# A chunked delta rule with two gated products: one row order, three inverse buffers, a lane inverse in one stream

## The chip, the core and the metric

The kernel runs on one core of a Trainium2 chip. The metric is the device time of one execution in microseconds; the time of a version is the median of several executions.

## What is computed

A delta-rule attention over 768 tokens for 4 x 8 pairs of batch and head (head size 48), then two dense products over its 3072 outputs of 384 numbers each.

```python
k_n = k / (norm(k, axis=-1) + 1e-06)
for t in range(768):
    y[t] = q[t] @ state
    v_old = k_n[t] @ state
    state = state + beta[t] * outer(k_n[t], v[t] - v_old)
xn = y / sqrt(mean(y * y) + 1e-6) * rms_g             # 3072 x 384
g = xn @ w_gate                                       # 384 x 1536
x = (silu(g) * (xn @ w_val)) @ w_out
h = x @ w_in                                          # 384 x 2048
out = (h * tanh(softplus(h))) @ w_out2
```

## The kernel before, in words

**Rows and segments.** The 768 tokens are cut into 12 rows `r` of 64 tokens, for all 32 pairs at once; two rows make a segment `sg`. In a row the recurrence is solved in closed form: a 64x64 unit-triangular matrix made of Gram products of the keys is inverted for each pair, and the row then needs matrix products alone. The state goes from row to row, so the rows follow each other. All this stands in `phase_b1`, which takes the first 510 us of the span. The two dense products behind it (phases b2 and c) are not edited.

**A row of the chain** (`chain_row`, L769). Its pieces have letters, and a table of letters gives their order on the engines:
- `r` `residual`: PE multiplies keys and state (L795), DVE subtracts that from v (L800).
- `q0`, `q1` turn q (PE L495, copied by ACT L496). `y` `of_state` is q by state (PE L813).
- `p` `scores`: q by keys (PE L478 into two PSUM banks), which DVE masks into `PT` (L487).
- `v` `values`: the inverse `A` by the residual (PE L832); ACT copies the result (L837).
- `k` `kv_update`: keys by values (PE L881); DVE adds them to the state `sx` (L886).
- `o0`, `o1` `outputs`: ACT, then POOL take mean square and root. Their other half belongs to the next row: `S`, `T` scale the output (`po`, DVE L893), `X`, `Y` (`to_x`) turn it on PE (L908), ACT copies it to `xh` and `xf` (L910, L913), and POOL makes the rest `xl` (L914). The tile of `xh` and `xl` is what the first dense product reads.
- `nA` is the norm of a later row's keys (square on ACT L418, sum `ss` on DVE L420, root `nr` on POOL L433 and L434); `nB` takes the reciprocal `rn` on DVE (L443) and scales the keys on POOL (`kh`, L444).
- `c0`, `c1` turn the normalized keys of row r+3 and `g` makes their Gram product into `A` (PE L478, masked by DVE L487); `d0`, `d1` and `h` do the same for row r+4.

Even rows follow `EVEN`, in which no `c`, `d`, `g`, `h` stands; odd rows follow `ODD`, which holds two Gram products; rows 0 and 1 have tables of their own.

**The inverse.** `inlane(sg)` (L499) inverts the 32x32 diagonal blocks of a segment's two rows at once on DVE, with some of the products on POOL (`prp`, both at L529). ACT and POOL copy the result into `A` (L601, L602). `merge32` (L608) then joins two 32-blocks to a 64-block by two PE products. `invert(sg)` runs `inlane` and then two `merge32`. It starts in an even row and ends in the next odd row; `PREP` and `SPLIT` say how much of it goes to which row. There are two `A` buffers; `As[sg % 2]` is taken again when `values` of row r-3 has read it.

**Part A** (`gated`, L205) is the first dense product for the first two of its pairs of weight slices, done beside the chain on the row before: nine-matmul pieces `up` (PE L201 to L203, the second matmul of each three reads `xl`), a gate on ACT, DVE and POOL (`sg` L242, `hh` L245, `hl` L246), and `down` (PE L218 to L220), whose sums ACT copies to `par` (L971).

**What sets the order.** `merge` (L32) interleaves the streams of a row (its chain, a budget of Part A given by `DUE`, weight conversions, the lane) by their planned weights; every engine then runs its instructions in the order in which they were issued. A wait on one engine so holds all that was issued behind it there.

Of the kernel before, what the change touches and what calls it, by code (L numbers as in the profile page):

```python
# [19 lines left out]
P = dict(  # L20
    XB=2, WE=16, RB=4, TB=3, PREP=42.0, SPLIT=0.40, XL=1, HH=0, DPRE=5, WU0=24, WU1=35, WARM=[0, 0], CVS=[2.6, 10.0, 2.5, 13.1, 0], CVA=12, CVT=12.22, CVB0=0, CVB1=1.238, CVC=2.31, PSD=1, INV=1, Q=[0, 2.7, 1.2, 9.9, 0, 18.8, 2.8, 3.0, 11.5, 10.6, 11.0, 19.4], W=[22, 2, 14, 8, 0, 14], SQ=1, QC=1, CVP=0, NE=2, BQ=3, NU=6, CVN=1, CVE=14.671, CVD=4.076, OFF=2.9, SOFT=0,
    EVEN="r nA S q0 T q1 X Y y v p nB k o0 o1".split(),
    ODD="r nA S q0 T q1 X Y y c0 v nB c1 p k g d0 o0 d1 o1 h".split(),
    R0="r q0 q1 p nA v o0 o1 s0 nB k s1 x0".split(),
    R1="r nA q0 Y q1 y p c0 v c1 nB k o0 o1 s1 g s0 d0 d1 x0 h".split(),
    DUE=[0, 4, 9, 10, 12],
    PRE="n2 t00 t01 w1 g0 s1 w2 s2 n3 t10 | t11 c g1 c c s3 t20 t21 | t30 g2 t31 w3 g3".split(),
# [31 lines left out]
def kernel(  # L59
# [133 lines left out]
    def need(*keys):  # L193
        assert done.issuperset(keys), set(keys) - done
# [72 lines left out]
    def phase_b1():  # L267
# [39 lines left out]
        kTs = [(kp if i in late_kT else il).tile([128, B, 2, 128], F32, name=f"kT{i}") for i in range(4)]  # L307
        As = [(kp if i == (NSEG - 1) % 2 else il).tile([128, 32, 64], F32, name=f"A{i}") for i in range(2)]
        qp = kp.tile([128, 16, 64], F32, name="qp")
# [151 lines left out]
        def products(r, soft=False):  # L461
            if r >= NR:
                return
            sg, rl = divmod(r, 2)
            if rl == 0:
                need(*([("v", r - 3)] if sg > 1 else []))
                A_t[sg] = As[sg % 2]
            need(("T", r, 0), ("T", r, 1))
            gram(("G", r), kT_t[r], kT_t[r], mneg, A_t[sg][:, rl * 16:rl * 16 + 16, :], soft, swap=True)
            yield 1  # L470
# [288 lines left out]

        def invert(sg):  # L760
            yield from inlane(sg)
            yield from delay(P["INV"])
            X11 = X11_t.pop(sg)
            Z = N_[:, 0:1024].rearrange("p (u c) -> p u c", c=32)
            for rl in range(2):
                us = slice(rl * 16, rl * 16 + 16)
                yield from merge32(2 * sg + rl, X11[:, us], Z[:, us])

        def chain_row(r):  # L769
# [129 lines left out]
            def to_x(bp):  # L899
# [154 lines left out]
        )  # L1054
        PREP = P["PREP"]
        SP = P["SPLIT"]
        M1A = 4.0 * FA + KD
        ps_ds = [ps_d]
        part_a = gated((ps_u, ps_ds, hp, tp), range(FA), range(NR), get_xa, finish_a, next_x)
        for sg in range(NSEG):  # L1060
            nxt = invert(sg + 1) if sg + 1 < NSEG else None
            for rl in range(2):
                r = 2 * sg + rl
                streams = [(chain_row(r) if r else chain0, cost(r))]
                due = P["DUE"][r] if r < len(P["DUE"]) else P["DUE"][-1 if r % 2 == 0 else -2]
                if due > 0:
# [208 lines left out]
```

## Time and profile before

| | |
|---|---|
| median of 3 runs | 1247.69 us (1244.75 to 1249.08) |
| profiled execution, its own time | 1247.47 us |
| its span | 1245.7 us |
| first phase, the chain's rows | to 510 us of the span |
| PE busy | 1118.6 us (90%) |
| DVE busy | 741.8 us (60%) |
| ACT busy | 510.1 us (41%) |
| POOL busy | 519.1 us (42%) |
| mean granted clock of TensorE | 0.934 of full speed |

Shares over the whole span mix two different parts. Behind 510 us the work is PE's alone; ahead of it PE and DVE take turns in setting the pace. So the rows below are cut by row of the chain. A row r begins with `residual` on PE: row 2 at 146.5 us, row 3 at 172.1, row 4 at 212.6, row 6 at 281.8, row 7 at 312.0, row 8 at 350.0, row 9 at 379.6, row 10 at 415.6. Where a timeline row ends in brackets, these hold the engine's idle time ahead of the instruction and what ended it.

### The profile page before, as it was taken

The numbers are of one execution on the slowest core, as the hardware profiler recorded it, in microseconds if no ns is written. First come the engines' busy times: TensorE is split into PE (matmuls) and PEld (weight loads), VectorE is DVE, ScalarE is ACT, GpSimd is POOL, SyncE is SP. The second block draws the span as 40 slices with busy tenths as digits, with TensorE's granted clock in tenths as the row PEclk, the third lists the DMA queues.
The fourth block names the chain that finished last, engine by engine and source line by source line (L and its number), as shares of the span: only waits on it lengthen the run. The fifth ranks groups of instructions, "written<-read, shape, count | busy, mean of one in ns | idle before, by whom it ended". The sixth has DMA issues, their size and how long they took to land.

```text
span 1245.7 us, 32276 instructions
## 1 busy us (share of the span) xinstructions
PE 1118.6 (90%) x14100; PEld 1083.2 (87%) x14100; DVE 741.8 (60%) x1133; ACT 510.1 (41%) x902; POOL 519.1 (42%) x441
## 2 busy tenths in 40 slices
PE   6575679888898887899999999997999999999998
PEld 5465568878787886899999999997999999999998
DVE  6999695868869598556555552269534333343333
ACT  3344324353443563221121110045655555565672
POOL 7256283655635355344434342234422322332232
PEclk9666689999999798899999999998999999999999
DMA  5224032333224354333343212332111011111101
GB/s 123 55 79 103 12 80 54 78 78 78 66 67 116 100 158 165 102 115 107 104 159 109 95 64 86 121 114 75 39 39 39 13 39 39 38 40 39 31 9 27
DMA packets 121438, 95.21 MB, mean 76 GB/s; under 512 B 80720, under 2 KB 103888, under 8 KB 121296
## 3 DMA queue, kind: packets, MB, share of 16 engines
q1 hardware_dynamic: 109200, 69.54, 19.8%
q10 hardware_dynamic: 12096, 23.60, 5.7%
q8 instruction: 111, 1.82, 0.6%
q14 instruction: 31, 0.25, 0.1%
HBM read 64.80 MB, written 28.31 MB: 75 GB/s over the span
## 4 chain that ended last, share of the span: by engine, by line
PE 69%; DVE 23%; issue 2%; ACT 2%; SPq 2%; POOL 1%; DMA 0%; DVEq 0%; POOLq 0%; ACTq 0%
PE pd L1171 5%; PE pd L1172 5%; PE pd L1170 5%; PE ph L201 5%; PE ph L202 5%; PE ph L203 5%; PE pv L201 4%; PE pd L218 4%; PE pg L201 3%; PE pd L219 3%; PE pg L203 3%; PE pg L202 3%; PE pd L220 3%; PE pv L203 3%; PE pv L202 3%; DVE pr L529 3%
## 5 line engine op out<-in xcount | busy, mean ns | idle before, releaser
L1218 POOL TENSOR_TENSOR gl<-t,gh 128x512 fp32r<-128x512 f32 x96 | 125.4, 1307 | 253.7 <-DVE gh L1217 252.3
L246 POOL TENSOR_TENSOR hl<-sg,hh 128x512 fp32r<-128x512 f32 x72 | 101.5, 1409 | 179.4 <-DVE hh L245 176.3
L201 PE MATMUL ph<-xh,wih 128*128 128x256 f32 x576 | 162.6, 282 | 4.6 <-DVE t L1214 4.6
L202 PE MATMUL ph<-xl,wih 128*128 128x256 f32 x576 | 162.4, 282 | 0.0
L203 PE MATMUL ph<-xh,wil 128*128 128x256 f32 x576 | 162.2, 282 | 0.0
L236 ACT ACTIVATE sg<-pg 128x512 f32<-128x512 f32 x72 | 43.1, 598 | 255.0 <-PE pg L203 218.0
L242 DVE TENSOR_TENSOR sg<-sg,pv 128x512 f32<-128x512 f32 x72 | 49.5, 687 | 151.6 <-PE pv L203 149.2
L218 PE MATMUL pd<-hh,woh 128*128 128x256 f32 x432 | 126.5, 293 | 7.7 <-ACT par L971 4.2
L1171 PE MATMUL pd<-wql,gh 128*128 128x384 f32 x384 | 130.4, 340 | 1.8 <-POOL wql L159 1.8
L1170 PE MATMUL pd<-wqh,gh 128*128 128x384 f32 x384 | 130.1, 339 | 1.7 <-DVE wqh L158 1.7
L1172 PE MATMUL pd<-wqh,gl 128*128 128x384 f32 x384 | 130.0, 339 | 0.0
L201 PE MATMUL pv<-xh,wvh 128*128 128x256 f32 x432 | 128.3, 297 | 0.0
L201 PE MATMUL pg<-xh,wgh 128*128 128x256 f32 x432 | 128.0, 296 | 0.0
L202 PE MATMUL pg<-xl,wgh 128*128 128x256 f32 x432 | 123.9, 287 | 2.5 <-POOL xl L914 2.5
L219 PE MATMUL pd<-hl,woh 128*128 128x256 f32 x432 | 123.2, 285 | 0.8 <-POOL hl L246 0.8
L203 PE MATMUL pv<-xh,wvl 128*128 128x256 f32 x432 | 123.9, 287 | 0.0
L202 PE MATMUL pv<-xl,wvh 128*128 128x256 f32 x432 | 123.8, 287 | 0.0
L203 PE MATMUL pg<-xh,wgl 128*128 128x256 f32 x432 | 123.8, 287 | 0.0
L220 PE MATMUL pd<-hh,wol 128*128 128x256 f32 x432 | 123.1, 285 | 0.0
L1214 DVE TENSOR_TENSOR t<-t,ph 128x512 f32<-128x512 f32 x96 | 65.2, 679 | 82.4 <-ACT t L1212 82.4
L201 PEld LDWEIGHTS ph<-xh,wih 128*128 128x128 f32 x576 | 109.6, 190 | 4.8 <-DVE t L1214 4.8
L202 PEld LDWEIGHTS ph<-xl,wih 128*128 128x128 f32 x576 | 109.5, 190 | 0.0
(197 smaller groups left out, 2951.6 us busy)
## 6 DMA issues: line engine op xcount, KB each, us to landing
raw<-in_moe_w_out_dram SPq DMA_DIRECT2D x28, 384.0 KB
raw<-in_moe_w_in_dram SPq DMA_DIRECT2D x16, 384.0 KB
kh<-in_k_dram SPq DMA_DIRECT2D x24, 192.0 KB
qp<-in_q_dram SPq DMA_DIRECT2D x24, 192.0 KB
v<-in_v_dram SPq DMA_DIRECT2D x48, 96.0 KB
raw<-in_moe_w_gate_dram SPq DMA_DIRECT2D x12, 384.0 KB
raw<-in_moe_w_val_dram SPq DMA_DIRECT2D x12, 384.0 KB
xh_d<-xh SPq DMA_DIRECT2D x12, 384.0 KB
```

Of the source, the lines that this page charges most:

```text
L201: nc.tensor.matmul(ps[:, f, :], wh[:, kt, sl], xh[:, kt, :], start=(kt == 0), stop=False)
L202: nc.tensor.matmul(ps[:, f, :], wh[:, kt, sl], xl[:, kt, :], start=False, stop=False)
L203: nc.tensor.matmul(ps[:, f, :], wl[:, kt, sl], xh[:, kt, :], start=False, stop=(kt == KD - 1))
L218: nc.tensor.matmul(ps, wh[:, f, sl], hh[:, f, :], start=(i + f == 0), stop=False)
L219: nc.tensor.matmul(ps, wh[:, f, sl], hl[:, f, :], start=False, stop=False)
L220: nc.tensor.matmul(ps, wl[:, f, sl], hh[:, f, :], start=False, stop=last)
L246: nc.gpsimd.tensor_tensor(out=hl, in0=sg, in1=hh.bitcast(F32), op=ALU.subtract)
L1170: nc.tensor.matmul(ps, gh[:, f, sl], wh[:, f, :], start=(m + f == 0), stop=False)
L1171: nc.tensor.matmul(ps, gh[:, f, sl], wl[:, f, :], start=False, stop=False)
L1172: nc.tensor.matmul(ps, gl[:, f, sl], wh[:, f, :], start=False, stop=last)
L1214: nc.vector.tensor_tensor(out=t, in0=t, in1=ps, op=ALU.mult)
L1218: nc.gpsimd.tensor_tensor(out=gl, in0=t, in1=gh.bitcast(F32), op=ALU.subtract)
```

## The change

Four edits, all in `phase_b1`:
- One table `ROW` orders rows 2 to 11. Each row turns the keys of row r+4 and makes one Gram product, and `R0` and `R1` do the same. In `ROW`, `nB` stands ahead of `X` and `Y`, `scores` stands far ahead of `kv_update`, scaling (`S`, `T`) stands some pieces ahead of turning (`X`, `Y`), and `values` follows `Y`.
- Three `A` buffers: the one of segment sg is taken again when `values` of row r-5 has read it. `comp`, the first tile of the lane inverse, moves to another tag with two buffers, and `Z` of the merges gets a tile of its own.
- `invert` becomes `merges` and one generator `lanes`, which runs the lane inverses of segments 2 to 5 one behind the other. The merges of a segment are stepped while the next segment's lane runs. Each row takes `LANE` = 16 of the stream's planned weight; the share in row 9 is 23 with no budget.
- Part A's budget per row becomes 4, 9, and 11 in every row from 3 on; before, it was 4, 9, then 10 and 12 by turns. Its last stretch behind the chain is planned at 20.0 for 21.0. The second of two copies of the lane's result on ACT is issued without a pause.

```diff
-    EVEN="r nA S q0 T q1 X Y y v p nB k o0 o1".split(),
-    ODD="r nA S q0 T q1 X Y y c0 v nB c1 p k g d0 o0 d1 o1 h".split(),
-    R0="r q0 q1 p nA v o0 o1 s0 nB k s1 x0".split(),
-    R1="r nA q0 Y q1 y p c0 v c1 nB k o0 o1 s1 g s0 d0 d1 x0 h".split(),
-    DUE=[0, 4, 9, 10, 12],
+    ROW="r nA q0 q1 S p T y nB X Y v c0 c1 k o0 g o1".split(),
+    R0="r q0 q1 p nA v o0 o1 s0 nB k s1 x0 c0 c1 g".split(),
+    R1="r nA q0 Y q1 y p nB v k o0 o1 s0 s1 x0 c0 c1 g".split(),
+    DUE=[0, 4, 9, 11],
...
-                need(*([("v", r - 3)] if sg > 1 else []))
-                A_t[sg] = As[sg % 2]
+                need(*([("v", r - 5)] if sg > 2 else []))
+                A_t[sg] = As[sg % 3]
...
-            comp = il.tile([128, 32, 32], F32, tag="X11", name="comp")
+            comp = il.tile([128, 1024], F32, tag="pr", name="comp", bufs=2).rearrange("p (u c) -> p u c", c=32)
...
             nc.scalar.copy(A[32:64, :, 32:64], Yc[32:64])
             nc.gpsimd.tensor_scalar(out=A[:, :, 0:32], in0=Yc, scalar1=h0[:, 0:1], scalar2=None, op0=ALU.mult)
+            nc.scalar.copy(A[96:128, :, 32:64], Yc[96:128])
             X11_t[sg] = X11
-            yield 2.0
-            nc.scalar.copy(A[96:128, :, 32:64], Yc[96:128])
-            yield 1.1
+            yield 0.1
...
+        def lanes():
+
+            ending = iter(())
+            for sg in range(2, NSEG):
+                done_of, due = 0.0, 4.0
+                for w in inlane(sg):
+                    yield w
+                    done_of += w
+                    if done_of >= due:
+                        next(ending, None)
+                        due += 2.5
+                for _ in ending:
+                    pass
+                ending = merges(sg)
+            yield from delay(P["INV"])
+            yield from ending
...
-                c0=lambda: turn_k(r + 3, 0), c1=lambda: turn_k(r + 3, 1),
-                g=lambda: products(r + 3), h=lambda: products(r + 4),
-                d0=lambda: turn_k(r + 4, 0), d1=lambda: turn_k(r + 4, 1),
+                c0=lambda: turn_k(r + 4, 0), c1=lambda: turn_k(r + 4, 1), g=lambda: products(r + 4),
...
-                elif nxt is not None:
-                    streams.append((budget(nxt, PREP * SP) if rl == 0 else nxt, PREP * (SP if rl == 0 else 1 - SP)))
+                elif sg + 1 < NSEG:
+                    pace = P["LANE"] if r < NR - 3 else 99.0
+                    streams.append((budget(lane, pace), P["LANE"] if r < NR - 3 else P["LANE"] + 7.0))
```

Lines of the changed kernel are 13 higher from `chain_row` on (L921 is the turn of x, L845 `values`, L894 `kv_update`, L927 `xl`), and one lower up to the lane's copies into `A` (L200 to L202 are `up`, L245 `hl`, L432 and L433 `nr`, L443 `kh`, L528 `prp`).

PE, an odd row (row 5), around the second turn of x. In a row read `out<-in`; `po` is the scaled output, `pg` and `pv` are the sums of Part A's `up`, and `wgh_1500` and `wvh_1682` belong to the block that Part A is already working on. Before; the first piece on the x tile just turned is the one with `wgh_886`:

```order
L908 MATMUL pp<-ident,po 128x128 x3
L813 MATMUL pp<-sx,QT 64x48 x32
L201 MATMUL pg<-xh,wgh_1500 128x256
...
L495 MATMUL pp<-ident,kh_173 128x128 x4
L832 MATMUL pp<-v,A_179 64x48 x32
L201 MATMUL pv<-xh,wvh_1682 128x256
...
L881 MATMUL pp<-ve_182,kh_170 64x48 x16
L201 MATMUL pg<-xh,wgh_886 128x256
L202 MATMUL pg<-xl,wgh_886 128x256
L203 MATMUL pg<-xh,wgl_887 128x256
```

The same place in the change, where the first piece on the new x tile has `wgh_887`:

```order
L921 MATMUL pp<-ident,po 128x128 x3
L845 MATMUL pp<-v,A_181 64x48 x32
L200 MATMUL pg<-xh,wgh_887 128x256
L201 MATMUL pg<-xl,wgh_887 128x256
L202 MATMUL pg<-xh,wgl_888 128x256
```

Between the second turn of x and the first read of the new tile stood four blocks of the chain (state, values, scores, `kv_update`), a turn of keys in two halves and three pieces of Part A; now `values` alone stands between them.

POOL, an odd row (row 5), from the norm of the keys or the products on, before (`prp` are lane products, `kh_174` are the keys, `hl` is Part A's rest):

```order
L529 TENSOR_TENSOR prp<-X__168,T_3528 128x512
L529 TENSOR_TENSOR prp<-X__168,T_3528 128x256
L433 TENSOR_TENSOR nr<-ss,half 128x16
L434 TENSOR_SCALAR nr<-nr 128x16
L914 TENSOR_TENSOR xl<-xf,xh 128x3x128 x2
L444 TENSOR_TENSOR kh_174<-kh_174,rn 128x16x48
L246 TENSOR_TENSOR hl<-sg,hh 128x512
```

And in the change:

```order
L432 TENSOR_TENSOR nr<-ss,half 128x16
L433 TENSOR_SCALAR nr<-nr 128x16
L528 TENSOR_TENSOR prp<-X__168,T_3545 128x512
L528 TENSOR_TENSOR prp<-X__168,T_3545 128x256
L443 TENSOR_TENSOR kh_174<-kh_174,rn 128x16x48
L927 TENSOR_TENSOR xl<-xf,xh 128x3x128
L245 TENSOR_TENSOR hl<-sg,hh 128x512
L927 TENSOR_TENSOR xl<-xf,xh 128x3x128
```

The two halves of `xl` stood behind `nr`; they now stand behind the lane products and `kh`, and an `hl` stands between them.

POOL, an even row (row 4), from the root `nr` on, before:

```order
L433 TENSOR_TENSOR nr<-ss,half 128x16
L434 TENSOR_SCALAR nr<-nr 128x16
L914 TENSOR_TENSOR xl<-xf,xh 128x3x128 x2
L246 TENSOR_TENSOR hl<-sg,hh 128x512
L529 TENSOR_TENSOR prp<-N__167,X__168 128x512
L529 TENSOR_TENSOR prp<-X__168,T_3416 128x512
L444 TENSOR_TENSOR kh_173<-kh_173,rn 128x16x48
```

And in the change, with the lane's copy into `A` ahead:

```order
L601 TENSOR_SCALAR A_181<-yc,h_161 128x32x32
L432 TENSOR_TENSOR nr<-ss,half 128x16
L433 TENSOR_SCALAR nr<-nr 128x16
L443 TENSOR_TENSOR kh_173<-kh_173,rn 128x16x48
L927 TENSOR_TENSOR xl<-xf,xh 128x3x128
L528 TENSOR_TENSOR prp<-N__167,X__168 128x512
L245 TENSOR_TENSOR hl<-sg,hh 128x512
L927 TENSOR_TENSOR xl<-xf,xh 128x3x128
```

Here, too, `kh` now precedes both halves of `xl`, and a lane product and `hl` stand between the two. The copy into `A` belongs to the segment before; it stood at the end of an odd row.

## Rows read from the trace of the kernel before

**Rows 1.** Stretches: us; PE, PEld, DVE, ACT, POOL busy; PEclk, DMA, GB/s.
```profile
146.50:172.10 25.60, 23.39 (x449) 21.51 (x447) 22.88 (x37) 10.00 (x23) 16.11 (x10) 0.85 0.34 79
172.10:212.60 40.50, 33.29 (x863) 30.26 (x862) 29.17 (x35) 17.66 (x36) 24.12 (x21) 0.92 0.24 61
281.80:312.00 30.20, 26.61 (x490) 24.26 (x486) 24.80 (x38) 11.22 (x26) 15.91 (x11) 0.94 0.32 81
312.00:350.00 38.00, 32.74 (x866) 29.73 (x865) 27.30 (x33) 17.65 (x36) 22.24 (x20) 0.96 0.20 55
350.00:379.60 29.60, 26.51 (x493) 24.29 (x490) 23.73 (x38) 10.53 (x25) 12.49 (x11) 0.94 0.26 69
379.60:415.60 36.00, 29.80 (x723) 27.25 (x722) 23.54 (x25) 14.87 (x31) 15.40 (x14) 0.88 0.35 101
510.00:1245.70 735.70, 723.06 (x5491) 721.05 (x5489) 337.64 (x533) 297.54 (x447) 253.30 (x213) 0.99 0.22 69
```

**Rows 2.** Waits of PE, 146.5 to 415.6 us: us in total, times, longest.
```profile
PE pp L908 <- DVE po L893: 15.5, 4, 5.6
PE pp L881 <- DVE PT L487: 8.9, 5, 2.6
...
PE pp L478 <- DVE sx L886: 3.1, 3, 1.0
...
PE pp L908 <- DVE X__168 L532: 1.0, 2, 0.5
```

**Rows 3.** Timeline of PE, rows 6 and 7: start, duration, instruction.
```profile
281.77 1.15 PE L795 MATMUL pp<-sx,kT 64*64 64x48 f32 x64
...
295.07 1.15 PE L832 MATMUL pp<-v,A 64*64 64x48 f32 x64
...
297.40 1.16 PE L478 MATMUL pp<-QT,kT 64*64 64x64 f32 x64
...
303.71 1.54 PE L881 MATMUL pp<-ve,kh 64*64 64x48 f32 x62 [2.61 <-DVE PT L487]
...
312.00 1.15 PE L795 MATMUL pp<-sx,kT 64*64 64x48 f32 x64
...
316.79 1.03 PE L495 MATMUL pp<-ident,qp 128*128 128x128 f32 x8
...
321.49 0.87 PE L908 MATMUL pp<-ident,po 128*128 128x128 f32 x3 [3.67 <-DVE po L893]
```

**Rows 4.** A stretch of low clock behind a wait, columns as above.
```profile
236.00:239.40 3.40, 3.40 (x61) 3.08 (x52) 3.37 (x7) 0.00 (x0) 0.90 (x2) 0.50 0.19 38
```

**Rows 5.** Timeline of POOL, rows 6 and 7.
```profile
281.02 1.27 POOL L246 TENSOR_TENSOR hl<-sg,hh 128x512 fp32r<-128x512 f32 x1 [1.35 <-DVE hh L245]
...
288.93 3.21 POOL L433 TENSOR_TENSOR nr<-ss,half 128x16 f32<-128x16 f32 x1 [6.64 <-DVE ss L420]
...
292.59 2.09 POOL L914 TENSOR_TENSOR xl<-xf,xh 128x384 fp32r<-128x384 f32 x2
...
298.87 2.04 POOL L246 TENSOR_TENSOR hl<-sg,hh 128x512 fp32r<-128x512 f32 x1 [4.19 <-DVE hh L245]
300.86 1.48 POOL L529 TENSOR_TENSOR prp<-N__167,X__168 128x512 f32<-128x512 f32 x1
...
307.14 1.48 POOL L444 TENSOR_TENSOR kh<-kh,rn 128x768 f32<-128x768 f32 x1 [2.50 <-DVE rn L443]
...
317.71 4.24 POOL L529 TENSOR_TENSOR prp<-X__168,T 128x512 f32<-128x512 f32 x2 [0.72 <-DVE T L588]
```

**Rows 6.** Timeline of ACT, row 7: the copy into `A`.
```profile
336.44 1.04 ACT L601 COPY A<-yc 32x1024 f32<-32x1024 f32 x1 [5.08 <-DVE yc L599]
```

**Rows 7.** Timeline of DVE, row 6.
```profile
287.90 0.95 DVE L420 TENSOR_REDUCE ss<-sq 128x16 f32<-128x768 f32 x1 [0.56 <-ACT sq L418]
...
295.86 0.36 DVE L539 TENSOR_REDUCE X__168<-pr 128x28 f32<-128x196 f32 x1
```

**Rows 8.** Timeline of PE, row 2: a piece of Part A.
```profile
159.63 0.38 PE L202 MATMUL pg<-xl,wgh 128*128 128x256 f32 x1 [1.86 <-POOL xl L914]
```

More of the change, by code (lines that the diff above doesn't have):

```diff
@@ L20 @@
 P = dict(
-    XB=2, WE=16, RB=4, TB=3, PREP=42.0, SPLIT=0.40, XL=1, HH=0, DPRE=5, WU0=24, WU1=35, WARM=[0, 0], CVS=[2.6, 10.0, 2.5, 13.1, 0], CVA=12, CVT=12.22, CVB0=0, CVB1=1.238, CVC=2.31, PSD=1, INV=1, Q=[0, 2.7, 1.2, 9.9, 0, 18.8, 2.8, 3.0, 11.5, 10.6, 11.0, 19.4], W=[22, 2, 14, 8, 0, 14], SQ=1, QC=1, CVP=0, NE=2, BQ=3, NU=6, CVN=1, CVE=14.671, CVD=4.076, OFF=2.9, SOFT=0,
-    EVEN="r nA S q0 T q1 X Y y v p nB k o0 o1".split(),
-    ODD="r nA S q0 T q1 X Y y c0 v nB c1 p k g d0 o0 d1 o1 h".split(),
-    R0="r q0 q1 p nA v o0 o1 s0 nB k s1 x0".split(),
-    R1="r nA q0 Y q1 y p c0 v c1 nB k o0 o1 s1 g s0 d0 d1 x0 h".split(),
-    DUE=[0, 4, 9, 10, 12],
+    XB=2, WE=16, RB=4, TB=3, LANE=16.0, XL=1, HH=0, DPRE=5, WU0=24, WU1=35, WARM=[0, 0], CVS=[2.6, 10.0, 2.5, 13.1, 0], CVA=12, CVT=12.22, CVB0=0, CVB1=1.238, CVC=2.31, PSD=1, INV=1, Q=[0, 2.7, 1.2, 9.9, 0, 18.8, 2.8, 3.0, 11.5, 10.6, 11.0, 19.4], W=[22, 2, 14, 8, 0, 14], SQ=1, QC=1, CVP=0, NE=2, BQ=3, NU=6, CVN=1, CVE=14.671, CVD=4.076, OFF=2.9, SOFT=0,
+    ROW="r nA q0 q1 S p T y nB X Y v c0 c1 k o0 g o1".split(),
+    R0="r q0 q1 p nA v o0 o1 s0 nB k s1 x0 c0 c1 g".split(),
+    R1="r nA q0 Y q1 y p nB v k o0 o1 s0 s1 x0 c0 c1 g".split(),
+    DUE=[0, 4, 9, 11],
     PRE="n2 t00 t01 w1 g0 s1 w2 s2 n3 t10 | t11 c g1 c c s3 t20 t21 | t30 g2 t31 w3 g3".split(),
@@ L307, in phase_b1 @@
         kTs = [(kp if i in late_kT else il).tile([128, B, 2, 128], F32, name=f"kT{i}") for i in range(4)]
-        As = [(kp if i == (NSEG - 1) % 2 else il).tile([128, 32, 64], F32, name=f"A{i}") for i in range(2)]
+        As = [(kp if i == (NSEG - 1) % 3 else il).tile([128, 32, 64], F32, name=f"A{i}") for i in range(3)]
         qp = kp.tile([128, 16, 64], F32, name="qp")
@@ L758, in quick_products, with merges @@
             yield from m32
-        def invert(sg):
-            yield from inlane(sg)
-            yield from delay(P["INV"])
+        def merges(sg):
             X11 = X11_t.pop(sg)
-            Z = N_[:, 0:1024].rearrange("p (u c) -> p u c", c=32)
             for rl in range(2):
                 us = slice(rl * 16, rl * 16 + 16)
-                yield from merge32(2 * sg + rl, X11[:, us], Z[:, us])
+                Z = il.tile([128, 16, 32], F32, tag="Z", name="Z")
+                yield from merge32(2 * sg + rl, X11[:, us], Z)
+        def lanes():
[13 more added lines that the diff above has]
+            yield from ending
         def chain_row(r):
@@ L961, in order @@
         def order(r):
-            return P["R0"] if r == 0 else P["R1"] if r == 1 else P["ODD"] if r % 2 else P["EVEN"]
+            return P["R0"] if r == 0 else P["R1"] if r == 1 else P["ROW"]
         def cost(r):
@@ L1054, in phase_b1 @@
         )
-        PREP = P["PREP"]
-        SP = P["SPLIT"]
+        lane = lanes()
         M1A = 4.0 * FA + KD
@@ L1060, in phase_b1 @@
         for sg in range(NSEG):
-            nxt = invert(sg + 1) if sg + 1 < NSEG else None
             for rl in range(2):
@@ L1064, in phase_b1 @@
                 streams = [(chain_row(r) if r else chain0, cost(r))]
-                due = P["DUE"][r] if r < len(P["DUE"]) else P["DUE"][-1 if r % 2 == 0 else -2]
+                due = P["DUE"][r] if r < len(P["DUE"]) else P["DUE"][-1]
                 if due > 0:
@@ L1073, in phase_b1 @@
                 if r == 0:
-                    lane1 = seq(reset(), nxt)
+                    lane1 = seq(reset(), inlane(1), delay(P["INV"]), merges(1))
                     streams.append((budget(lane1, Q[8]), Q[8]))
@@ L1100, in phase_b1 @@
         wbp.append(st_w.enter_context(pool("wbB")))
-        merge((part_a, 21.0), (budget(cv, P["CVT"]), P["CVT"]))
+        merge((part_a, 20.0), (budget(cv, P["CVT"]), P["CVT"]))
         st_p.close()
```

## The prediction

> **What bounds the kernel now.** I read first the stretches by row of the chain. After 510 us, in the two MoE products, PE is busy 723.1 of 735.7 us [rows 1]; nothing there is edited, so only the first 510 us can change. In rows 2 to 9, where the lane inverse runs, PE is busy 23 to 33 us of each row and DVE 23 to 29; an even and an odd row together (row 6 and row 7) take 30.2 + 38.0 = 68.2 us, with DVE busy 24.8 + 27.3 = 52.1 [rows 1]. No engine is full, so I went to what PE waits for: from 146.5 to 415.6 us it waits 15.5 us for the scaled output `po`, 8.9 us for the masked scores `PT`, 3.1 us for the state `sx`, all three from DVE [rows 2]. In the program they stand at two places: in an even row `kv_update` comes right behind `scores` and waits 2.61 us for the bank that DVE empties; in an odd row `to_x` follows its scaling at once and waits 3.67 us, because DVE still does lane products [rows 3]. With 0.5 at the even row's second x turn and 1.0 at a Gram product [rows 2], 7.8 us of a pair go here. Each of the two long waits is followed by 3.4 us at a granted clock of 0.50, the lower level, 1.2 GHz, in which PE is busy throughout [rows 4]; half of that is lost, so 3.4 us per pair more. These 7.8 + 3.4 = 11.2 us of 68.2 are what the new order can win.
>
> **What it removes.** The new row order puts three or more PE pieces between `scores` and the next use of its banks, between scaling and turning, and between `kv_update` and the Gram product. Walking the DVE order of a pair with the durations of before (52.1 us of work), each of `po`, `PT`, `sx` is ready before PE gets there. I count the 7.8 us as gone.
>
> **What it adds: a wait for POOL.** Part A takes the x tile of the row before. In before, PE reads it first some 10 us after it is turned (odd row) or behind state, values and scores (even row). Now PE reads it right behind `values` (front matter, PE order): the second matmul of that `up` needs `xl`, which POOL makes. And POOL now has the normalization `kh` and the `hl` of the same row (and lane products) ahead of the second `xl`; before, both halves stood directly behind `nr` or the products. Time from the start of the row (`residual`):
> - Odd row, PE: residual 1.15 and the down product with its wait for `par` to 4.8 (start of `residual` to start of the turn of q), turn 1.03, five pieces of nine matmuls and the three blocks scores, state, values, each piece with a block 2.33 (values to scores), so 5.9 for the five pieces and 3.4 for the blocks, two x turns of 0.4 (three of q's eight transposes each) [rows 3]: x is wanted at +15.9; with part of the pieces' losses at the seams counted once, about +15.3, which I take.
> - Odd row, POOL: `ss` ends 7.1 us after the row's start in before (288.85 against 281.77) and cannot come earlier, since ACT's square stands behind the same down product. From there POOL does `nr` until the next can start 3.6, the pair of products 4.24, `kh` 1.48, `xl` 1.0, `hl` 1.27 to 2.04, `xl` 1.0 [rows 5]: 12.6, so `xl` at +19.7 to +20.5. The wait is 4.5 us.
> - Even row, POOL: ACT first copies the lane's result twice (1.04 each) [rows 6], so PE gets the down product's `par` 0.8 us late and `ss` starts at about +6.8. From `ss` to the last small lane product DVE took 287.90 to 296.22, 8.3 us [rows 7]; with the scores' mask 1.3 `rn` comes at +16.4. Then `kh` 1.48, `xl` 1.0, product 1.48, `hl` 1.3, `xl` 1.0: +22.8. PE is there at +19.3 (the odd row's sum with two merge blocks and the 0.8). The wait is 3.5 us.
>
> That PE waits just there when POOL is behind has one example in before: in row 2 the same matmul stands 1.86 us for `xl`, which POOL made late [rows 8].
>
> **The sum, against the profiled execution's 1247.47 us** (0.22 below the median of the runs):
> - Rows 4 to 7: per pair -7.8 + 0.8 + 3.5 + 4.5 = +1.0. The two long waits are near the old ones in length, so I leave the low-clock loss as it is. Two pairs: **+2**. Lower bound: `xl` comes right behind an `hl` that nothing holds up (0.4 and 1.7 us of wait) and the clock stays up: -4.9 - 3.4 = -8.3 per pair, -17. Upper: POOL's operations at their long durations, +7.4 per pair (below), +15.
> - Rows 2 and 3, 66.1 us: PE's idle 9.4 us [rows 1] go. Row 3 gets the odd row's 4.5. In row 2, x is wanted right behind its turn: residual, scores and state 3.4, turn of q 1.0, four pieces 4.8, x turn 0.4, and losses, about +10.3. `kh` comes first on POOL again, and its `rn` stands on DVE behind `ss` (+7), the masks 1.3, six small products (half of the 8.3 above), two conversion steps and `hh`: an estimate of +14.9; with `kh` and `xl` 1.48 + 1.0, x is there at +17.4: 7 us. Against that row 2's Gram product and turns are only moved. With a little more low clock: **+2.5** (-12 to +9, the ends being both waits at the 1.86 of [rows 8] or both prolonged by the long `hl` and one more low stretch).
> - Rows 8 and 9, 29.6 + 36.0 us: no later row needs `nr` and `kh`, so POOL is free and `xl` is on time. Of PE's idle 9.3 us [rows 1] some 5 remain, most at the end of row 9, where the last lane's result goes through ACT (2 x 1.04) before its merges: **-4** (-8 to 0).
> - Rows 0 and 1: a turn (1.03) and a Gram product (a block, 1.15 [rows 3]) move from row 1 into row 0, ahead of the quick lane's products there; their mask moves with them, so the two rows together keep their work on DVE, but DVE may wait for the product. **+1** (0 to +4.4, both exposed at half the clock).
> - Row 10 to the end: Part A's 112 pieces instead of 111 before the tail of 20 instead of 21. Same work: **0** (-2.5 to +2, a piece or two into or out of idle time).
> - Of no cost: the third `A` buffer, `comp` and `Z` in tiles of their own (the wait they lift, on the merges' reads, was not on PE's list [rows 2]); the A copy issued without pause; SP, whose order is unchanged, though v's loads stand behind the later `xl_d` store: they are wanted only at the next residual, over 10 us on.
>
> +2 + 2.5 - 4 + 1 + 0 = +1.5: **1249.0 us**, no change that can be measured (a measurement of this kernel tells about 0.3%, 3.7 us, from nothing). By itself this case runs from 1241 to 1257.
>
> **The rivals.**
> - *The waits go and nothing takes their place.* If POOL gets through `kh` and `hl` early enough, rows 4 to 7 take the lower bound, -17, rows 2 and 3 about -9, rows 8 and 9 -4, rows 0 and 1 +1: 1247.5 - 29 = 1218.5; I write 1220. A pair would take 60 us, still above DVE's 52.1. For it: POOL is busy only 15.9 + 22.2 = 38 of 68 us [rows 1], and the lane now feeds DVE and POOL evenly. Against it: what counts is not POOL's share but the chain from `ss`, and that cannot start sooner.
> - *Slower, by longer POOL operations.* In before `hl` takes 1.27 us beside a DVE mask that reads PSUM, and 2.04 us beside a lane product of two SBUF tensors; a lone product takes 1.48, the pair 4.24 [rows 5]. A continuous lane puts DVE products beside nearly all of POOL's work. With `hl` at its long time and the product a microsecond longer both waits pass 5 us, +3 per pair, and each then drags a second stretch of low clock, +3.4. Three pairs: 19 us on top of 1249, **1268**. It decides from the point where the wait is nearer to the 5.6 us of row 3 than to 3.67. The Trainium skill (GPSIMD Engine Reference, 1. Specifications) says that POOL's SBUF interfaces are shared with VectorE, with contention when a DVE instruction has two SBUF inputs; the two durations of `hl` agree with it. By that rule the time would be this rival's 1268. I still take the forecast's durations: in the new order much of POOL's work falls beside masks, reductions and an idle DVE.
> - *The change does not do what it says*: excluded but for a trifle, since the built order shows the Gram product in every row and the split `xl`.
>
> **Chances.** Forecast 0.50, gap-free 0.27, slower 0.20, no effect 0.03. Half of the forecast's own range lies within 3.7 us of 1247.5, a quarter on each side: same 0.25 + 0.03, faster 0.12 + 0.27, slower 0.13 + 0.20. The range takes in half of each rival: 1221 to 1266.
>
> **What would show it.** Right: PE's list of waits for rows 2 to 9 is headed by `pg <- POOL xl` with some 3 to 5 us once a row in rows 3 to 7, `po` and `PT` nearly gone from it; pairs of 67 to 71 us; low clock behind each such wait. Gap-free: that entry under 2 us a row and pairs near 60. Slower: waits over 5 us and `hl` at 2 us. It would be wrong altogether if DVE's masks (`A`, `sx`) headed the list at the start of a row: then the balance of PE and DVE, not POOL, sets the rows.

## The result, and the profile after

The changed kernel takes **1262.86 us** (median of 4 runs, 1260.37 to 1266.24) against 1248.38 us before (4 runs): the ratio is 1.012, its 95% interval 1.0085 to 1.0156. The change makes the kernel slower by 1.2%. Its profiled execution took 1260.37 us, with a span of 1258.7 us for 1245.7.

First the stretches by row of the chain, to be read beside [rows 1] (a stretch, its length, busy time of PE, PEld, DVE, ACT and POOL, granted clock, share of DMA, GB/s). They are rows 2, 3, 6, 7, 8, 9, and the two dense products:

```profile
152.70:185.80 33.10, 27.04 (x520) 24.72 (x519) 23.50 (x38) 10.99 (x25) 18.06 (x12) 0.80 0.26 61
185.80:222.50 36.70, 27.37 (x551) 25.26 (x550) 26.99 (x34) 10.41 (x24) 21.31 (x16) 0.91 0.26 66
...
294.40:331.90 37.50, 32.20 (x804) 30.08 (x802) 26.78 (x42) 17.86 (x37) 22.09 (x17) 0.91 0.26 66
331.90:366.20 34.30, 26.59 (x550) 24.64 (x546) 22.59 (x29) 11.07 (x27) 16.60 (x13) 0.90 0.23 60
366.20:396.10 29.90, 28.17 (x737) 26.00 (x733) 23.74 (x38) 16.69 (x36) 16.54 (x14) 1.00 0.26 69
396.10:428.40 32.30, 28.70 (x731) 26.10 (x730) 21.88 (x26) 15.92 (x33) 17.29 (x14) 1.00 0.39 113
523.00:1258.70 735.70, 722.45 (x5490) 720.05 (x5489) 338.94 (x533) 297.40 (x447) 253.65 (x214) 0.99 0.22 69
```

In the last 735.7 us of both spans PE runs as many instructions (5490 for 5491), so the dense products take as long as before. The even row 6 has grown from 30.2 to 37.5 us and the odd row 7 has shrunk from 38.0 to 34.3: the merges (256 matmuls) and one of the odd row's two Gram products (64) now stand in the even row. The pair went from 68.2 to 71.8. From the starts of `residual` in both traces:

| stretch | before, us | after, us | difference | forecast |
|---|---|---|---|---|
| start to row 2 | 146.5 | 152.7 | +6.2 | +1 |
| rows 2 and 3 | 66.1 | 69.8 | +3.7 | +2.5 |
| rows 4 to 7 | 137.4 | 143.7 | +6.3 | +2 |
| rows 8 and 9 | 65.6 | 62.2 | -3.4 | -4 |
| row 10 to the end | 830.1 | 830.3 | +0.2 | 0 |
| sum | 1245.7 | 1258.7 | +13.0 | +1.5 |

PE's waits in rows 3 to 7 (what waits, what for, us in total, times, longest) answer to [rows 2]:

```profile
PE pg L201 <- POOL xl L927: 29.6, 5, 7.3
PE pd L217 <- ACT par L982: 3.3, 5, 0.9
PE pp L808 <- DVE A L486: 1.6, 1, 1.6
```

`po`, `PT` and `sx` are gone from the list, and one entry has taken their place: the second matmul of the first piece on a new x tile, which waits for POOL's `xl` once in every row. Row 7 shows how (PE's timeline: start, duration, instruction, idle time ahead of it):

```profile
331.93 1.15 PE L808 MATMUL pp<-sx,kT 64*64 64x48 f32 x64
...
345.13 1.15 PE L845 MATMUL pp<-v,A 64*64 64x48 f32 x64
...
353.85 0.58 PE L201 MATMUL pg<-xl,wgh 128*128 128x256 f32 x1 [7.25 <-POOL xl L927]
```

PE is through with `values` and the first matmul of the new piece at 346.6 us and then has nothing to do for 7.25 us. POOL in the same stretch, to be read beside [rows 5]:

```profile
339.08 4.55 POOL L432 TENSOR_TENSOR nr<-ss,half 128x16 f32<-128x16 f32 x1 [5.11 <-DVE ss L419]
343.72 2.07 POOL L433 TENSOR_SCALAR nr<-nr 128x16 f32<-128x16 f32 x1
345.87 2.39 POOL L528 TENSOR_TENSOR prp<-X__168,T 128x512 f32<-128x512 f32 x2
348.23 1.47 POOL L443 TENSOR_TENSOR kh<-kh,rn 128x768 f32<-128x768 f32 x1
349.66 1.97 POOL L927 TENSOR_TENSOR xl<-xf,xh 128x384 fp32r<-128x384 f32 x1
351.59 1.25 POOL L245 TENSOR_TENSOR hl<-sg,hh 128x512 fp32r<-128x512 f32 x1
352.81 0.98 POOL L927 TENSOR_TENSOR xl<-xf,xh 128x384 fp32r<-128x384 f32 x1
```

The second `xl` ends at 353.79, and PE starts at 353.85. All that POOL does from 339.08 on is on the path: `nr` 4.55 and 2.07 us, two lane products, `kh`, `xl`, `hl`, `xl`.

### The profile page after: what moved, and what is told of

Same layout as the page of the kernel before. It is cut to its first block, busy times and chain, and to the rows that moved or that the text cites. A ratio compares the mean times of both kernels' runs of the same rounds, so it can differ in the third digit from the quotient of the medians.

```text
span 1258.7 us, 32278 instructions
## 1 busy us (share of the span) xinstructions
PE 1117.9 (89%) x14100; PEld 1084.4 (86%) x14100; DVE 735.5 (58%) x1133; ACT 510.2 (41%) x902; POOL 524.6 (42%) x441
## 4 chain that ended last, share of the span: by engine, by line
PE 62%; DVE 6%; issue 1%; POOL 1%; ACT 1%; ACTq 0%; DVEq 0%; POOLq 0%
PE pd L1181 5%; PE pd L1182 5%; PE pd L1180 5%; PE ph L200 5%; PE ph L201 5%; PE ph L202 5%; PE pd L217 4%; PE pd L219 3%; PE pg L201 3%; PE pd L218 3%; PE pg L200 3%; PE pg L202 3%; PE pv L200 3%; PE pv L202 3%; PE pv L201 3%; DVE t L141 2%
## 5 line engine op out<-in xcount | busy, mean ns | idle before, releaser
L200 PE MATMUL ph<-xh,wih 128*128 128x256 f32 x576 | 162.7, 283 | 4.9 <-DVE t L1224 4.9
L201 PE MATMUL pg<-xl,wgh 128*128 128x256 f32 x432 | 128.7, 298 | 40.8 <-POOL xl L927 40.8
L202 PE MATMUL ph<-xh,wil 128*128 128x256 f32 x576 | 162.4, 282 | 0.0
L245 POOL TENSOR_TENSOR hl<-sg,hh 128x512 fp32r<-128x512 f32 x72 | 96.3, 1337 | 147.0 <-DVE hh L244 140.3
L200 PE MATMUL pg<-xh,wgh 128*128 128x256 f32 x432 | 130.7, 303 | 0.6 <-ACT xh L923 0.6
L202 PE MATMUL pg<-xh,wgl 128*128 128x256 f32 x432 | 127.1, 294 | 0.0
L200 PE MATMUL pv<-xh,wvh 128*128 128x256 f32 x432 | 126.5, 293 | 0.5 <-issue 0.5
L201 PEld LDWEIGHTS pg<-xl,wgh 128*128 128x128 f32 x432 | 87.7, 203 | 42.9 <-POOL xl L927 42.9
L202 PE MATMUL pv<-xh,wvl 128*128 128x256 f32 x432 | 122.2, 283 | 0.0
L200 PEld LDWEIGHTS ph<-xh,wih 128*128 128x128 f32 x576 | 109.8, 191 | 5.1 <-DVE t L1224 5.1
```

Source lines behind the costliest of these rows:

```text
L200: nc.tensor.matmul(ps[:, f, :], wh[:, kt, sl], xh[:, kt, :], start=(kt == 0), stop=False)
L201: nc.tensor.matmul(ps[:, f, :], wh[:, kt, sl], xl[:, kt, :], start=False, stop=False)
L202: nc.tensor.matmul(ps[:, f, :], wl[:, kt, sl], xh[:, kt, :], start=False, stop=(kt == KD - 1))
L245: nc.gpsimd.tensor_tensor(out=hl, in0=sg, in1=hh.bitcast(F32), op=ALU.subtract)
```

## The experiments

Theory 1 was that the place of `xl`, on POOL behind `nr`, `kh` and `hl` and on PE ahead of Part A's first read, makes the loss. Theory 2 was that the continuous lane fills DVE and POOL, so that the waits would turn up elsewhere whatever the order. All runs are compared with the kernel before on the same chip (ratios), and with the 1262.86 us of the changed kernel. The chips differ from run to run; the kernel before had medians of 1247.97 to 1249.79 us on them, so a difference of times between two runs is good to some 2 us.

### kh behind xl

```diff
-    ROW="r nA q0 q1 S p T y nB X Y v c0 c1 k o0 g o1".split(),
+    ROW="r nA q0 q1 S p T y X Y nB v c0 c1 k o0 g o1".split(),
```

> One letter moved in the changed kernel's row table: nB (rn and kh) stands behind X and Y, so on POOL both halves of xl come ahead of kh, and in odd rows ahead of hl too. Theory 1 (PE waits because kh and hl stand ahead of xl in POOL's queue): PE's wait for xl falls from 3.8 to 4.4 us to under 1 us in even rows and from 7 us to some 3.6 us in odd rows (nr and the pair of products stay ahead of it there); rows 2 to 7 give back 20 to 25 us, about 1240 us. Theory 2 (the continuous lane makes POOL's and DVE's operations long, whatever their order): the waits keep their sum to within a third, 1255 us or more.

1256.55 us (ratio 1.0064, 1.0049 to 1.0079), 6 us back instead of the 20 to 25 expected. Its waits of PE in rows 3 to 7:

```profile
PE pp L494 <- POOL kh L443: 10.4, 5, 2.4
PE pg L201 <- POOL xl L927: 10.4, 5, 2.9
```

The 29.6 us for `xl` fell to 10.4, as theory 1 had it, but as much came up at the turn of the keys, which now waits for `kh`. POOL in an odd row of this kernel:

```profile
343.26 1.95 POOL L927 TENSOR_TENSOR xl<-xf,xh 128x384 fp32r<-128x384 f32 x2
345.16 2.26 POOL L245 TENSOR_TENSOR hl<-sg,hh 128x512 fp32r<-128x512 f32 x1
347.39 1.47 POOL L443 TENSOR_TENSOR kh<-kh,rn 128x768 f32<-128x768 f32 x1
```

`kh` starts behind both halves of `xl` and `hl`, and the turn of the keys stands on PE one piece of Part A behind the wait for `xl`. So the order of `kh` and `xl` matters less than the expectation had it: both are wanted soon, and both hang on the same chain from `ss`. Of theory 2, that a wait only changes its place was right for this edit.

### Part A three pieces later

```diff
-    DUE=[0, 4, 9, 11],
+    DUE=[0, 3, 7, 11],
...
-        merge((part_a, 20.0), (budget(cv, P["CVT"]), P["CVT"]))
+        merge((part_a, 23.0), (budget(cv, P["CVT"]), P["CVT"]))
```

> Part A runs some three pieces later in the changed kernel (its budgets 3, 7, 11 instead of 4, 9, 11, its last stretch planned at 23 instead of 20), so that the first piece on a new x tile comes at the end of a row, four pieces and kv_update behind the second turn of x. Nothing on POOL or DVE is taken out. Theory 1 (the place of the first read of xl decides): no wait for xl is left in rows 2 to 9, 34 us of waits and some 8 us of low clock go, 3 to 4 us come back in the last stretch and a few us turn up elsewhere: 1225 to 1235 us. Theory 2 (POOL and DVE are what is full): the waits turn up at other places, 1250 us or more.

**1220.97 us** (ratio 0.9769, 0.9741 to 0.9797), a few us below what theory 1 gave. Waits of PE from row 3 into row 9, and the stretches of an even and an odd row:

```profile
PE pp L494 <- POOL kh L443: 6.7, 3, 2.3
PE pp L921 <- DVE po L906: 3.9, 2, 3.2
PE pp L808 <- DVE A L486: 1.6, 2, 1.4
```

```profile
267.90:297.40 29.50, 29.50 (x804) 27.70 (x802) 25.07 (x41) 17.77 (x37) 21.36 (x15) 1.00 0.33 83
297.40:326.30 28.90, 26.70 (x550) 24.74 (x546) 24.27 (x30) 11.29 (x27) 18.57 (x15) 0.94 0.26 71
```

No wait for `xl` is left, with not one instruction of POOL or DVE taken out. The even row has PE busy throughout at the full clock; a pair takes 58.4 us for 71.8. Theory 2 falls. The wait for `kh`, 2.2 us in each odd row, is what remains.

The same shift in the kernel before:

```diff
-    DUE=[0, 4, 9, 10, 12],
+    DUE=[0, 3, 7, 10, 12],
...
-        merge((part_a, 21.0), (budget(cv, P["CVT"]), P["CVT"]))
+        merge((part_a, 24.0), (budget(cv, P["CVT"]), P["CVT"]))
```

> The kernel before with Part A three pieces later (budgets 3, 7 for 4, 9 in rows 1 and 2, its last stretch 24 for 21), the edit that took the changed kernel from 1263 to 1221 us. Theory 1 (the change pays, and its price is the early read of xl alone): before has no waits for xl, so the shift is worth little here, 1243 to 1252 us. Theory 3 (the shift is an improvement of its own, whatever the row order): 1235 us or below.

1250.59 us (ratio 1.0011, 0.9999 to 1.0023): worth nothing there. So the 42 us between 1262.86 and 1220.97 are the price of reading x too early in the new order, and not a gain that the shift brings by itself.

### The chain from ss to xl

Two edits of the changed kernel shorten that chain: nA stands first in a row, or the second operation of `nr` is left out (the 1e-6 is not added to the norm).

```diff
-    ROW="r nA q0 q1 S p T y nB X Y v c0 c1 k o0 g o1".split(),
+    ROW="nA r q0 q1 S p T y nB X Y v c0 c1 k o0 g o1".split(),
```

> The changed kernel with nA ahead of r in the row table, so that ACT squares the keys ahead of the copies of the down product, and the chain ss, nr, products, kh, xl can start some 3 to 4 us earlier in a row. Theory 1 (the chain from ss to xl on POOL sets PE's wait): the waits for xl fall by 2.5 to 4 us each, to about 0 to 1 us in even and 3 to 4 us in odd rows: 1238 to 1248 us. Theory 2 (the sum of POOL's and DVE's work is full): the waits stay within 1 us of 4 and 7, 1258 us or more.

1256.02 us (ratio 1.0052, 1.0036 to 1.0068). The waits in rows 3 to 7 fell from 29.6 us to

```profile
PE pg L201 <- POOL xl L927: 21.3, 5, 5.5
```

which is 1.7 us each, less than theory 1 expected; the time lies between the two cases written down. The wait in row 2 even rose, from 4.6 to 6.0 us. DVE and POOL in row 7 of this kernel show why the waits fell so little:

```profile
340.11 1.52 DVE L528 TENSOR_TENSOR pr<-X__168,T 128x768 f32<-128x768 f32 x1
341.54 0.25 DVE L442 RECIPROCAL rn<-nr 128x16 f32<-128x16 f32 x1
```

```profile
342.01 1.48 POOL L443 TENSOR_TENSOR kh<-kh,rn 128x768 f32<-128x768 f32 x1 [2.52 <-PE pp L921]
```

`kh` starts 0.22 us behind the end of the reciprocal `rn`, which DVE takes up only behind a lane product; POOL stood idle 2.52 us there. (The bracket names PE's turn of x. That `kh` waited for `rn` is read from the times: in the next run the bracket names another PE instruction, and `kh` again starts 0.22 us behind `rn`.) The chain matters, and DVE has a part in it.

```diff
-            nc.gpsimd.tensor_scalar(out=nr, in0=nr, scalar1=1e-6, scalar2=None, op0=ALU.add)
```

> The changed kernel without the second operation of nr, the addition of 1e-6 on POOL (left out of the computation). In odd rows that operation on 16 numbers takes 2.07 us for 0.26 in even rows, and it starts just as a DVE product of two SBUF tensors begins. If POOL's operation is held up by DVE's, the next POOL operation (a lane product) is held up in its place and PE's wait for xl in odd rows falls by 0.3 to 0.7 us: 1261 to 1263 us. If the operation is long by itself, the wait falls by 2 us in rows 3, 5 and 7: 1255 to 1258 us.

1262.16 us, no gain (ratio 1.0107, 1.0089 to 1.0125), though the waits for `xl` in rows 3, 5 and 7 fell by 1.2, 0.8 and 1.1 us, to 6.1. In the same rows PE now waits for the scaled output, which it had not:

```profile
PE pp L920 <- DVE po L905: 2.5, 3, 0.8
```

What the operation had cost on POOL came up on DVE. First DVE in row 7 of the changed kernel, from `ss` on, then DVE without the operation:

```profile
338.05 0.95 DVE L419 TENSOR_REDUCE ss<-sq 128x16 f32<-128x768 f32 x1 [2.11 <-ACT sq L417]
338.92 1.94 DVE L528 TENSOR_TENSOR pr<-X__168,T 128x1024 f32<-128x1024 f32 x1
340.77 0.62 DVE L906 SCALAR_TENSOR_TENSOR po<-po,rv,gB 128x384 f32<-128x384 f32 x1
...
343.62 0.62 DVE L906 SCALAR_TENSOR_TENSOR po<-po,rv,gB 128x384 f32<-128x384 f32 x1
344.14 1.52 DVE L528 TENSOR_TENSOR pr<-X__168,T 128x768 f32<-128x768 f32 x1
345.82 0.25 DVE L442 RECIPROCAL rn<-nr 128x16 f32<-128x16 f32 x1 [0.16 <-POOL nr L433]
```

```profile
337.88 0.95 DVE L419 TENSOR_REDUCE ss<-sq 128x16 f32<-128x768 f32 x1 [2.11 <-ACT sq L417]
...
343.45 1.95 DVE L905 SCALAR_TENSOR_TENSOR po<-po,rv,gB 128x384 f32<-128x384 f32 x1
345.32 2.03 DVE L527 TENSOR_TENSOR pr<-X__168,T 128x768 f32<-128x768 f32 x1
347.27 0.24 DVE L441 RECIPROCAL rn<-nr 128x16 f32<-128x16 f32 x1
```

And POOL without it:

```profile
343.44 2.57 POOL L527 TENSOR_TENSOR prp<-X__168,T 128x512 f32<-128x512 f32 x2
347.73 1.48 POOL L442 TENSOR_TENSOR kh<-kh,rn 128x768 f32<-128x768 f32 x1 [1.72 <-PE pp L844]
```

In the changed kernel DVE's `po` and lane product take 0.62 and 1.52 us, and POOL's `nr` on 16 numbers takes 2.07 beside them; it ends 0.13 us after the DVE product. Without that `nr` POOL's lane product starts 0.01 us ahead of `po`, and now `po` takes 1.95 us and the product 2.03. `rn` starts 8.4 us behind the end of `ss` for 6.8, and `kh` 8.9 behind it for 9.2: little is won on the chain, and the waits for `po` take it back. Neither of the two outcomes written down ahead came quite: POOL's next operation was not held up, DVE's was.

### Rows 0 and 1

```diff
-    R0="r q0 q1 p nA v o0 o1 s0 nB k s1 x0 c0 c1 g".split(),
-    R1="r nA q0 Y q1 y p nB v k o0 o1 s0 s1 x0 c0 c1 g".split(),
+    R0="r q0 q1 p nA v o0 o1 s0 nB k s1 x0".split(),
+    R1="r nA q0 Y q1 y p c2 v c3 nB k o0 o1 s1 g2 s0 c0 c1 x0 g".split(),
```

Here `c2`, `c3` and `g2` are the turn and the product of row r+3.

> Rows 0 and 1 of the changed kernel get their old order back (Gram product of row 4 in row 1, beside that of row 5), all else stays. If the product and the turn moved into row 0 cost what the traces differ by there (6.2 us by the start of row 2), about 1257 us; if those 6.2 us come from Part A's earlier wait for xl in row 1 alone (3.2 us for 0.7), about 1260 us; if rows 0 and 1 don't matter, 1263 us.

1257.83 us (ratio 1.0079, 1.0061 to 1.0097). Row 2 starts at 147.4 us for 152.7, so the 5 us are made in rows 0 and 1: 1.8 in row 0, which loses the turn and the product, and 3.4 in row 1, though that row gets them back. There PE waits 0.6 us for `xl` instead of 3.2, and its other waits are shorter, too. So the first case written down has the time, but the product and the turn are not the whole reason; the early read of x has a part in it.

### What the parts of the change are worth

The buffers alone in the kernel before, without the rest:

```diff
-                A_t[sg] = As[sg % 2]
+                A_t[sg] = As[sg % 3]
...
-            comp = il.tile([128, 32, 32], F32, tag="X11", name="comp")
+            comp = il.tile([128, 1024], F32, tag="pr", name="comp", bufs=2).rearrange("p (u c) -> p u c", c=32)
...
-            Z = N_[:, 0:1024].rearrange("p (u c) -> p u c", c=32)
+                Z = il.tile([128, 16, 32], F32, tag="Z", name="Z")
```

> The kernel before with three A buffers, comp and Z in tiles of their own, and nothing else of the change. Both theories: the buffers by themselves lift no wait that stands on PE's list, 1246 to 1250 us. If the lane's later start on a free buffer is worth something by itself, under 1244 us.

1247.45 us (ratio 0.9986, 0.9975 to 0.9997): 0.1%, as good as nothing. The changed kernel with the lane planned as before:

```diff
-                    streams.append((budget(lane, pace), P["LANE"] if r < NR - 3 else P["LANE"] + 7.0))
...
+                    streams.append((budget(nxt, PREP * SP) if rl == 0 else nxt, PREP * (SP if rl == 0 else 1 - SP)))
```

> The changed kernel with the lane inverse planned as before: per segment one inverse with its merges behind it, 0.40 of it in the even row, the rest in the odd row; row order, three A buffers and Part A's budgets stay as changed. Theory 1 (order of POOL's queue and Part A's first read): PE still waits for xl in every row from 3 to 7, 3 us or more, 1255 to 1275 us. Theory 2 (the continuous stream is to blame): the waits for xl fall under 2 us and the time is at 1250 us or below.

1269.43 us (ratio 1.0169, 1.0154 to 1.0184), 6.6 us slower than the changed kernel, with the waits for `xl` still there (26.4 us in rows 3 to 7). The stream is not to blame. The same with Part A later, where no wait for `xl` hides what the stream is worth:

> The changed kernel with Part A three pieces later, and with the lane inverse planned as before (0.40 of a segment in the even row, the rest with its merges in the odd row), so that the two runs with and without the stream stand beside each other where no wait for xl is left. If the row order alone brings the gain, 1219 to 1226 us. If the even load of the stream is part of it (DVE's work of an odd row is longer than PE's without it), 1230 to 1245 us: the waits for DVE's scaled output po come back in odd rows.

1255.08 us (ratio 1.0043, 1.0024 to 1.0062), outside both expectations: 34 us worse than with the stream. An odd row and an even row:

```profile
247.20:291.70 44.50, 37.74 (x806) 34.67 (x802) 27.75 (x35) 17.94 (x36) 22.00 (x18) 0.81 0.22 56
291.70:318.20 26.50, 25.40 (x550) 23.35 (x546) 22.06 (x35) 11.11 (x26) 17.30 (x12) 1.00 0.36 92
```

The merges stand in the odd row again (806 PE instructions for 550), which takes 44.5 us at a clock of 0.81, and the even one takes 26.5; the pair is back at 71.0 us. PE waits 6.7 us in the odd row, 3.4 of them for `po`, and from 276.4 to 289.9 us it works without a gap at a granted clock of 0.50, the lower level. What keeps the clock down so long was not followed further. Last, the stream and the buffers with the four row tables of before, and Part A later:

```diff
-    ROW="r nA q0 q1 S p T y nB X Y v c0 c1 k o0 g o1".split(),
+    EVEN="r nA S q0 T q1 X Y y v p nB k o0 o1".split(),
+    ODD="r nA S q0 T q1 X Y y c0 v nB c1 p k g d0 o0 d1 o1 h".split(),
...
-    DUE=[0, 4, 9, 11],
+    DUE=[0, 3, 7, 10, 12],
```

> The kernel before with the lane inverse as one stream, three A buffers and Part A three pieces later, so that beside the run of the changed kernel with Part A later (1221 us) only the row tables differ. If the even load of the stream is what pays, 1219 to 1230 us. If the row order is needed too (its products in every row, and pieces between scaling and turning, between scores and kv_update), PE's waits for po and PT and the long odd rows stay: 1238 to 1250 us.

1239.83 us (ratio 0.9911, 0.9878 to 0.9944). The waits of before are back, from row 2 into row 9:

```profile
PE pp L922 <- DVE po L907: 18.8, 7, 8.9
PE pp L895 <- DVE PT L487: 4.8, 1, 4.8
```

So with Part A later the four combinations are 1250.6 us (old order, old lane), 1239.8 (stream alone), 1255.1 (order alone), 1221.0 (both). The two need each other: the stream gives 11 us in the old order and 34 in the new one. (The old order has its own tables for rows 0 and 1, which were worth 5 us above. So what the order does alone, 5 us worse, may be these tables; what the stream gives is compared under the same tables each time.)

### A version that beats both

Both candidates take Part A later and rows 0 and 1 as of old. In the first nA also stands ahead of r:

> The changed kernel with Part A three pieces later, rows 0 and 1 in their old order, and nA ahead of r, the turn of keys at its place. Theory 1: kh comes some 3 us earlier, so the waits of 2.2 us for it go as well: 1205 to 1215 us. If the reciprocal rn behind DVE's lane products sets kh, as the run with nA first shows in part, half of it stays: 1212 to 1218 us.

1216.44 us (ratio 0.9732, 0.9706 to 0.9758), within the second case: from row 2 to row 10 PE still waits 4.4 us for `kh`, and 13.2 us for `po`. In the second candidate the turn of the keys goes behind `kv_update` instead:

```diff
-    ROW="r nA q0 q1 S p T y nB X Y v c0 c1 k o0 g o1".split(),
+    ROW="r nA q0 q1 S p T y nB X Y v k c0 c1 o0 g o1".split(),
```

> The changed kernel with Part A three pieces later, rows 0 and 1 in their old order, and the turn of keys (c0, c1) behind kv_update in the row table. Theory 1 (waits at the first reads are what is left): rows 0 and 1 give 5 us against 1221 us, the waits of 2.2 us for kh in odd rows and 1.7 us of low clock behind each go: 1205 to 1213 us. If DVE or POOL is full by now, the wait for kh turns up at the Gram product and only the 5 us of rows 0 and 1 come: 1215 to 1218 us.

**1207.78 us** (ratio 0.9663, 0.9633 to 0.9692), 3.4% faster than before and within the first case. Rows 3 to 8 in one stretch, then PE's one long wait there:

```profile
173.70:343.90 170.20, 165.38 (x3978) 154.19 (x3976) 151.40 (x209) 85.87 (x186) 119.81 (x89) 0.98 0.32 82
```

```profile
PE pp L808 <- DVE A L486: 3.3, 1, 3.3
```

PE is busy 165.38 of 170.20 us at a clock of 0.98. One long wait is left, 3.3 us for DVE's mask of `A` at the start of row 3; behind it PE hardly stops until row 9. DVE, busy 151.40, would come next; no run tries that.

## Why the prediction was right and wrong

**Right: what goes and what comes.** The waits for `po`, `PT` and `sx` left the list, as counted, and one wait for `xl` a row took their place. Pairs of 71.9 and 71.8 us stand just above the 67 to 71 written down. The range, 1221 to 1266, holds the time.

**Wrong: the likeliest case.** It said no measurable change, and the kernel is 1.2% slower. The time lies between that forecast (1249) and the rival that ends slower (1268), nearer to the rival. Two terms of the sum were too small.

*Rows 4 to 7, +2, measured +6.3.* The step that failed is the wait of the odd row, put at 4.5 us and measured at 6.92 and 7.25; the even row's, put at 3.5, came to 3.78 and 4.36. In row 7 the start of the chain was right (`ss` ends 7.1 us after the row's start, as taken). `nr` was taken as 3.6 us from its start to the next operation, from a row [rows 5] in which DVE did mostly small products; it took 6.8. The pair of products was taken as 4.24 and took 2.36; the first `xl` took 1.93 for 1.0; PE came at +14.7 instead of +15.3. That is +3.2 - 1.9 + 0.9 + 0.6 = +2.8 us, which makes 4.5 into 7.3.

The even row's wait came out near the forecast by luck: in row 6 `xl` was there at +22.9 for the +22.8 written down, but `rn` had ended at +15.0 instead of +16.4, and POOL's operations behind it took longer than taken (`kh` 2.10 for 1.48, the second `xl` 1.85 for 1.0). The low clock, which the sum left as it was, also grew: behind the even rows' waits PE worked 5.4 us at 0.50 where 3.4 were taken, half of which is lost, so 1 us per pair. In all the four waits came 6.3 us above their forecast and the low clock 2, of which some 4 were saved again, most of it in PE's busy time at the full clock.

*Rows 0 and 1, +1, measured +6.2.* Only the product and the turn were priced, at up to 4.4, which is less than what came. That row 1, too, has a first read of a new x tile, which had waited 0.7 us before and now waits 3.2, was not in the sum, though the forecast had the same wait in every later row.

**The slower rival.** Its mechanism came, at another instruction. It had `hl` at 2.04 us; `hl` took 1.25 in row 7, and `nr` was the operation that grew, from 3.6 to 6.8 us. The Trainium skill (Trainium Architecture — The Big Picture, What this means for kernel authors) says that VectorE and GpSimd share a port pair to SBUF under an exclusive lock; the rows agree, in both directions: the second `nr` took 2.07 us in row 7 beside DVE's `po` and lane product for 0.26 in row 6, and DVE's `po` 1.95 for 0.62 when POOL came first. Of its price, a wait above 5 us in every row was right for odd rows alone, and the low clock was not doubled: 3.4 us as before behind the odd rows' waits, 5.4 behind the even rows'.

**The gap-free rival** was put at 1220 us. It was wrong for this change. With the early read lifted and nothing else, the kernel ran at 1220.97, but that the two agree so well is partly luck: rows 4 to 7 were then 116.9 us for the 120.4 of the rival, and rows 2 and 3 60.7 for 57.1. Nor is 1220 a bound, since the last version above ran at 1207.78.

**The small terms.** Rows 8 and 9 (-4, measured -3.4), row 10 to the end (0, +0.2) and the buffers (nothing, 0.1% alone) came as forecast. In rows 2 and 3 (+2.5, measured +3.7) two errors met: row 2 waited 4.6 us where 7 were taken, and row 3 waited 7.25 for 4.5. (The lower end written there, -12, does not follow from both waits at 1.86, which give some -6.)

What stays open: how much of the odd row's 7 us is the held-up port and how much the order on DVE ahead of `rn`; the runs moved one into the other and didn't part them.

## What to carry to other kernels

When a new order takes waits out of a list, look for the first read of everything that the same engines make a little later. Here waits of 7.8 us a pair went, and 10.7 to 11.6 us a pair came, at a read for which `xl` had stood ready some 4 us (row 6) and 7 us (row 7) ahead. Where a wait stands at a chain with several links, giving the reader more to do first (three pieces of other work: 42 us) paid far more than shortening one link (6 us, 7 us, nothing). And two edits can need each other: with Part A later the even lane and the even rows gave 11 and -5 us alone (the -5 may be the tables of rows 0 and 1), 30 together.

## What the hardware showed that was not expected

The second `nr`, an operation on 16 numbers a lane, took 2.07 us on POOL in rows 3 and 7, in which DVE was in `po` and a lane product, both of SBUF tensors, and 0.26 us in row 6. In row 5, where it ended behind `po` alone, it took 0.64, and the two lane products behind it took 3.50 for 2.39. The delay is mutual: with the operation taken out on POOL, it came up as 1.3 us more on DVE's `po` and 0.5 more on the lane product behind it.

A wait's length didn't set what it cost in clock behind it. Around the 7.25 us wait of row 7 (stretch, length, busy times, granted clock, DMA, GB/s):

```profile
346.60:349.90 3.30, 0.00 (x0) 0.00 (x0) 3.23 (x6) 1.63 (x4) 3.30 (x4) 1.00 0.30 117
350.00:353.80 3.80, 0.00 (x0) 0.00 (x0) 0.78 (x1) 0.00 (x0) 3.79 (x3) 0.51 0.00 0
353.85:357.20 3.35, 3.35 (x17) 3.35 (x18) 0.00 (x0) 0.39 (x1) 0.00 (x0) 0.55 0.65 178
```

PE is idle throughout the first two stretches; the granted clock is 1.00 in the first and 0.51, the lower level, in the second, and 0.55 in the third, where PE works on. Some 3.4 us of slow work follow here, as they followed the waits of 2.6 us [rows 4] and 3.7 us before. What of the low clock falls into the wait costs nothing, for PE does nothing there. Behind the shorter waits of the even rows, 3.78 us in row 4 and 4.36 in row 6, the slow work was longer, 5.4 us; why was not followed:

```profile
245.60:251.00 5.40, 5.40 (x25) 5.36 (x25) 0.69 (x1) 1.17 (x2) 3.58 (x3) 0.50 0.60 149
317.30:322.70 5.40, 5.39 (x25) 5.39 (x25) 0.69 (x1) 1.17 (x2) 3.66 (x3) 0.50 0.58 146
```
